# x rows staged in U's memory, W kept split in scratch, and loads placed steps ahead of their splits in a two-layer FNet and H3 kernel

## The chip, the cores and the metric

The kernel runs on one core of one Trainium2 chip. The metric is the device time of one execution in microseconds. The kernel before took 1289.1 us (median of 3 runs, 1285.89 to 1290.16).

## The reference

Two kinds of sublayer alternate, each with a residual and a layer norm in front: an FNet mixing layer (a) and a gated long convolution (b). S = 2048, D = 576, all float32.

```
x = x + A(layernorm(x));  x = x + B(layernorm(x), k, v, ...)     # twice

def A(x):                                   # Real(DFT_seq(DFT_hidden(x)))
    a = x @ dft_hid_re.T;  b = x @ dft_hid_im.T
    return dft_seq_re @ a - dft_seq_im @ b

def B(q):
    k_shift = causal 4-tap depthwise convolution of k with shift_k
    kv = k_shift * v
    y = long causal convolution of kv with ssm_k over S (by FFT of length 2S)
    return q * (y + kv * ssm_D)
```

B's convolution depends on k, v and weights alone, so it is the same in both rounds and is computed once.

## The kernel before, in words

Rows are laid out as 16 tiles j of 128 partitions x 576. Matrix products must be nearly float32 exact: every operand is split into a high part h (ScalarE, an ACTIVATE that rounds to float32r) and a low part l (VectorE, a subtraction: `split`, lines 76 to 78), and a product is three matmuls, hh, hl and lh. All matmuls are recorded under line 63, all such splits under lines 77 and 78; other lines name themselves. TensorE (PE) runs 6320 matmuls, of 512 or 288 columns.

The order is made by a list scheduler that places instructions on the five in-order engine queues from the program's order and its own estimates. SyncE (SP) issues nearly all loads and stores, in order: a load that must wait for a free buffer holds back everything behind it on that queue. `load_after` (line 128) only keeps a load behind an earlier one.

**First A layer** (`layer`, lines 265 to 301, called at 555): 128 steps n = (tb, g, k), 4 blocks tb of 512 output columns, g the real or imaginary sequence matrix C, k the 16 row tiles. A step is 14 matmuls: 12 into four accumulators s and 2 into rm for the last 64 columns of D. C tiles (256 KB) are loaded and split two steps ahead (`load_c`). In the first 16 steps the row tiles X[k] are made as they are needed: `load_x` (509) loads x into the ring "res", which has two slots of 576 words in `flts`; `get_x0` (514) asks for row j+1, takes the layer norm of row j (statistics on VectorE for the first eight rows, lines 141 to 155; on ScalarE for the others, 495 to 505; the power -0.5 on POOL) and splits it into X[j] (`to_x`, 157: rounding at line 159, low part at 161 and 162). After steps 15 and 31 and so on the accumulators are split into U, nine tiles of the transformed block in their own part `UT` of the tile `mats` (`evac_u`, `evac_r`). `hidden` (241) then multiplies U with the nine chunks of the hidden matrix W: 27 matmuls of 288 columns per half row tile, 216 for a block's four row tiles. Its pieces are spread over the steps after W_END, one a step (`finish`).

**Beside it** runs `branch` (310), the convolution of B, paced by `want` (556 to 561) in pieces per step: F1 (32 items, ssm_k and kv for 16 j, 12 matmuls each, steps 0 to 42; the kv items are eight VectorE operations, 363 to 366), with results stored to DRAM (`t_d`); then the middle stage (64 groups, lines 404 to 452, 9 matmuls each), which reads `t_d` and writes `v_d`; then I2 (16 items, to step 112). F1 takes the memory regions A and B; W lives in region A afterwards, so `load_w` (197) fills it between F1's end and the hidden products, in steps 41 to 46, from two "res" slots. `copy_w` (188) copies W to DRAM scratch in steps 47 to 55, unsplit.

**Second A layer**: rows of the second layer are made in steps 113 to 127 (`get_x1`, 525). Its first block of 512 columns is again 32 steps (counted 128 to 159 below). In steps 144 to 159 `build` (602) makes sums of rows for the other three blocks, from y reloaded from DRAM (`build_load`, 593): four kp, each in four pieces (tiles T5, T6, T7, T4 and R), one piece a step, its loads one step ahead. The other three blocks use Strassen's scheme (`strassen`, 706): seven products m in the order 5, 1, 6, 2, 7, 3, 4, four steps kp each, C combinations loaded four steps ahead. All four blocks' U goes to DRAM (`u_d`). In the last Strassen block, at the end of a product, W is reloaded and split into freed rows of X, and U of blocks 0 and 1 is loaded and split into freed places (`load_u`, 687; loops at 792 to 798). Then the tail (802 to 807): four blocks of hidden products with the final gate and output (`gated`, 487), U of block tb + 2 loaded and split behind block tb.

Of the kernel before, what the change touches and what calls it, by code (L numbers as in the profile page):

```python
# [10 lines left out]
F32 = mybir.dt.float32  # L11
FR = mybir.dt.float32r
AF = mybir.ActivationFunctionType
OP = mybir.AluOpType
# [16 lines left out]
F1_END = 40  # L31
W_END = 46
MID_END = 96
# [5 lines left out]
WIDE = 2 * NT  # L39
KR = 4  # L40
STAT = 20
STATIC = 14
B_LOAD = 15
B_FROM = 16
CSB = 5
U_AT = J * 2 * D
C_AT = U_AT + 9 * WIDE
RT_AT = 8 + 4 * STAT
# [5 lines left out]
def fnet_h3_kernel(ctx: ExitStack, tc: tile.TileContext, x, c_mat, w_re, w_im, k_pad, v, shift_k,  # L54
# [29 lines left out]
    def flat(words, dt, name):  # L84
        return sb.tile([P, words], dt, tag=name, name=name)
# [31 lines left out]

    mats = flat(C_AT + 3 * WIDE, FR, "mats")
    xs = mats[:, :U_AT].rearrange("p (j n) -> p j n", j=J)
    UT = mats[:, U_AT:C_AT].rearrange("p (k a n) -> p k a n", k=9, a=2)  # L120
    flts = flat(FLT, F32, "flts")
    mhalf = flts[:, :1]
    lay(flts, 8, ("stat", STAT, 4), ("rt", NT, 1))
    lay(mats, C_AT, ("cs", WIDE, 3))
# [62 lines left out]

    def copy_w():
        for ch in range(9):
            if ch < 8:  # L190
                load_after(w_d[ch], (w_re if ch < 4 else w_im)[(ch % 4) * P:(ch % 4 + 1) * P, :])
            else:
                load_after(w_d[ch][:REM], w_re[NC * P:, :])
                load_after(w_d[ch][REM:], w_im[NC * P:, :])
            yield

    def load_w(im_sign, late=False):
        W.clear()
        for ch in range(9):
            if not late and ch == 0:  # L200
                wg = region_a(FR, "w").rearrange("p (k n) -> p k n", k=9)
            w = two(xs[:, ch] if late else wg[:, ch])
            if late:
                load_after(w[:, 1].bitcast(F32), w_d[ch])
                split_in(w[:, 0], w[:, 1])
            else:
                raw = ring["res"]()
                if ch < 8:
                    nc.sync.dma_start(raw, (w_re if ch < 4 else w_im)[(ch % 4) * P:(ch % 4 + 1) * P, :])
                else:  # L210
                    nc.sync.dma_start(raw[:REM], w_re[NC * P:, :])
                    nc.sync.dma_start(raw[REM:], w_im[NC * P:, :])
                for lo, hi, sg in ((0, P, 1 if ch < 4 else im_sign),) if ch < 8 else ((0, REM, 1), (REM, P, im_sign)):
                    if sg > 0:
                        split(w[lo:hi, 0, :], w[lo:hi, 1, :], raw[lo:hi])
                    else:
                        nc.scalar.activation(w[lo:hi, 0, :], raw[lo:hi], AF.Copy, scale=-1.0)
                        nc.vector.scalar_tensor_tensor(w[lo:hi, 1, :], raw[lo:hi], -1.0,
                                                       w[lo:hi, 0, :].bitcast(F32), op0=OP.mult,
                                                       op1=OP.subtract)  # L220
            W.append(w)
            yield

    U = {}

    def evac_u(g, ps, dc):
        u = UT[:, g * NC + dc]
        split(u[:, 0, :], u[:, 1, :], ps[dc])
        U[g * NC + dc] = u

    def evac_r(g, ps):
        if g == 0:
            U[8] = UT[:, 8]
# [76 lines left out]
    def branch():  # L310
        wt = []
        f1r = region_b(FR, "f1r")
        lay(f1r, 0, ("xf", 2 * D, 3), ("fc", 4 * P, 3))
        lay(flts, SC_AT + 3 * NT + 3 * D, ("so", D, 3))
        f1f = region_a(F32, "f1f")
        lay(f1f, 0, ("k", 2 * D, KR), ("wt", 2 * D, 2), ("tmp", D, 1), ("v", D, 2), ("land", D, 3))

# [68 lines left out]
        for j, src in todo:  # L386
# [5 lines left out]
            yield  # L392
        f1_products(*xf)
        m1 = region_b(FR, "mid")
        lay(m1, 0, ("df", 2 * D, 3), ("yf", D, 3), ("mc", 4 * P, 1))
        fresh("res")
        lay(flts, SC_AT + 3 * NT, ("res", D, 2), ("kk", D, 2), ("pp", D, 1), ("vo", HD, 3))
# [111 lines left out]
    def load_x(j):  # L509
        if j < J:  # L510
            XL[j] = ring["res"]()
            nc.sync.dma_start(XL[j], x[:, j, :])
# [27 lines left out]
    pending = []  # L540
    lay(flts, SC_AT, ("craw", NT, 3), ("res", D, 2), ("junk", D, 1))
    br = branch()
    wl, wc = load_w(-1), copy_w()
    load_x(0)
    if PRE == 1:
        get_x0(0)
    for used in range(1, K_FIRST + 1):
# [7 lines left out]
    for n in layer(get_x0, lambda j: x[:, j, :], done0, pending):  # L555
        if n <= F1_END:
            want = K_FIRST + (F1_16 * n // 16 if n <= 16 else F1_16 + (32 - K_FIRST - F1_16) * (n - 16) // (F1_END - 16))
        elif n <= MID_END:
            want = 32 + 64 * (n - F1_END) // (MID_END - F1_END)
        else:  # L560
            want = min(113, 96 + 17 * (n - MID_END) // (I2_END - MID_END))
# [8 lines left out]
        if W_END < n <= W_END + 9:  # L570
            next(wc, None)
        m = n - PREP
        if m == 0:
            lay(flts, SC_AT + 3 * NT + 2 * D, ("xa", D, 2), ("yb", D, 2))
            lay(region_b(F32, "gate"), 0, ("xa", D, 3), ("yb", D, 3))
        if 0 <= m < TB * (TB - 1):
            get_x1(m)
    T, R, t7 = {}, {}, []

    def t_slot(m, kp):  # L580
        n = 4 * (m - 4) + kp
        return mats[:, U_AT + n * WIDE:U_AT + (n + 1) * WIDE] if n < 9 else t7[0][:, (n - 9) * WIDE:(n - 8) * WIDE]

# [17 lines left out]

    def build(kp, halves, rems):
        (b11, b12), (b21, b22) = ((t[:, :, :H], t[:, :, H:]) for t in halves)
        nc.vector.tensor_tensor(b22, b22, b12, OP.subtract)
# [6 lines left out]
        keep(7, kp, b22)  # L611
        nc.vector.tensor_tensor(rems[1], rems[1], rems[0], OP.subtract)
        t = two(t7[0][:, 7 * WIDE + kp * 4 * REM:7 * WIDE + (kp + 1) * 4 * REM])
        split(t[:, :, :REM], t[:, :, REM:], rems[1])
        R[kp] = t
        yield
# [69 lines left out]

    def load_u(tb, chs):
        for ch in chs:
            at = hu_slots[tb % 2][ch]
            t = two(t_slot(*at) if ch < 3 or tb % 2 == 0 else xs[:, at, :2 * NT])  # L690
            load_after(t[:, 1, :].bitcast(F32), u_d[tb][ch])
            split_in(t[:, 0, :], t[:, 1, :])
            HU[tb, ch] = t

# [73 lines left out]
    for n in layer(get_x1, lambda j: xb_d[j], done1, pending, 1):  # L768
        finish(pending, 1)
        if n == STATIC:  # L770
# [12 lines left out]
            ring["cs"].tiles.extend([free, *held])  # L783
        if n >= B_LOAD and (n - B_LOAD) % 4 == 0 and len(loaded) < KP:
            loaded.append(build_load(len(loaded)))
# [6 lines left out]
    wl = load_w(1, True)  # L792
    for tb, m, kp in strassen():
        if tb == TB - 1 and kp == KP - 1:
            for _ in range({1: 4, 6: 4, 3: 1}.get(m, 0)):
                next(wl)
            load_u(0, {6: range(4), 2: range(4, 8), 7: (8,)}.get(m, ()))
            load_u(1, {7: range(3), 3: range(3, 9)}.get(m, ()))
# [82 lines left out]
```

## Time and profile before

| What | Value |
|---|---|
| Median of 3 runs | 1289.1 us (1285.89 to 1290.16) |
| Profiled execution, its own time | 1285.66 us |
| Its span, first to last instruction | 1283.8 us |
| Mean granted TensorE clock | 0.983 |
| PE busy | 1210.0 us (94%), 6320 matmuls |
| DVE / ACT busy | 866.5 us (67%) / 634.4 us (49%) |
| DMA moved | 252.97 MB, mean 197 GB/s |
| W loads (9 + 1 transfers), each | 288 KB, 3.7 to 4.2 us to landing |
| U reloads | 256 KB, 5.2 to 5.4 us to landing |
| Reload of W from scratch | 9 of 288 KB, 4.9 us to landing |

A row of the profile's groups or waits names engine and line: "PE s L63 <- ACT mats L159" is PE, about to write s, released by ScalarE's instruction of line 159 that wrote mats; then the total, the number of times and the longest, in us. A timeline row has start, length, engine, line, operation, out<-in, shapes, count, and in brackets the idle time of the engine before it with what ended it. "q" behind an engine is its sequencer, where DMAs are issued. Matmul ends are modelled, and a busy PE may be a slow one.

### The profile page before, as it was taken

The page shows a single profiled execution, that of the slowest core. Times are in us where ns is not written, and L with a number is a line of the kernel's source. Part 1 is how long each engine was busy: PE and PEld are TensorE (multiplying, and loading weights), DVE is VectorE, ACT ScalarE, POOL GpSimd, SP SyncE. Part 2 cuts the span into 40 slices and gives each one's busy share as a digit, 9 for nine tenths or more (in the row PEclk, how much of TensorE's full clock was granted, in tenths as well). Part 3 has the DMA queues.
Part 4 walks back from the last instruction along what each step waited for, and adds up shares of the span by engine and source line. Part 5 has one row for each costly group of instructions (what it writes and reads, how often), then busy time and mean ns, then how long its engine had stood idle before and what let it go on. Part 6 is the DMA issues. An engine that isn't in the chain of part 4 may idle for free.

```text
span 1283.8 us, 18285 instructions
## 1 busy us (share of the span) xinstructions
PE 1210.0 (94%) x6320; PEld 1038.0 (81%) x6320; DVE 866.5 (67%) x1596; ACT 634.4 (49%) x1255; POOL 73.8 (6%) x102
## 2 busy tenths in 40 slices
PE   6689999999999999999998899999999999989997
PEld 5468888798789987788887788788877777779997
DVE  6867888547885588783257865665667667774664
ACT  4475565727884588874364332434443444560110
POOL 1110000000000000000012311000000000000111
PEclk9789999999999999999999999999999999999999
DMA  9557988736544455536798853675375476496631
GB/s 317 181 163 233 310 261 260 252 130 201 153 138 134 143 161 151 159 117 219 235 296 283 265 192 131 211 240 166 105 253 181 118 254 209 158 306 208 207 136 46
DMA packets 140670, 252.97 MB, mean 197 GB/s; under 512 B 15361, under 2 KB 39937, under 8 KB 140418
## 3 DMA queue, kind: packets, MB, share of 16 engines
q1 hardware_dynamic: 101698, 200.42, 49.3%
q10 hardware_dynamic: 33984, 42.48, 9.4%
q0 software_dynamic: 4896, 8.92, 2.6%
q8 instruction: 49, 0.80, 0.3%
q14 instruction: 43, 0.35, 0.1%
HBM read 190.42 MB, written 64.00 MB: 198 GB/s over the span
## 4 chain that ended last, share of the span: by engine, by line
PE 65%; DMA 11%; DVE 9%; ACT 8%; issue 3%; POOL 2%; SPq 0%; ACTq 0%; POOLq 0%; DVEq 0%
PE s L63 33%; PE bk L63 26%; PE rm L63 5%; DMA ph<-in_c_mat 3%; DMA t<-flts 2%; ACT mats L77 2%; DVE mats L78 1%; POOL flts L148 1%; ACT mid L77 1%; DVE flts L145 1%; DMA flts<-in_c_mat 1%; DMA mid<-t 1%; DMA flts<-in_x 1%; ACT flts L438 1%; ACT flts L419 1%
## 5 line engine op out<-in xcount | busy, mean ns | idle before, releaser
L63 PE MATMUL s<-mats 128*128 128x512 f32 x2292 | 589.3, 400 | 31.9 <-ACT mats L159 19.4
L63 PEld LDWEIGHTS s<-mats 128*128 128x128 f32 x2292 | 430.9, 192 | 123.5 <-ACT mats L159 22.5
L77 ACT ACTIVATE mats<-flts 128x512 fp32r<-128x512 f32 (+1 forms) x225 | 140.2, 626 | 163.8 <-PE rm L63 105.4
L78 DVE TENSOR_TENSOR mats<-flts,mats 128x512 fp32r<-128x512 f32 (+1 forms) x225 | 153.6, 685 | 58.7 <-ACT mats L77 57.2
L63 PEld LDWEIGHTS bk<-mid 128*128 128x128 f32 x768 | 111.4, 189 | 34.6 <-ACT flts L438 10.4
L63 PE MATMUL bk<-mid 128*128 128x288 f32 x768 | 126.2, 302 | 13.1 <-ACT flts L438 4.4
L63 PE MATMUL bk<-w,mats 128*128 128x288 f32 x864 | 121.6, 295 | 1.1 <-ACT flts L438 0.9
L63 PEld LDWEIGHTS bk<-w,mats 128*128 128x128 f32 x864 | 117.9, 188 | 3.6 <-ACT flts L438 1.4
L78 DVE TENSOR_TENSOR mid<-mid 128x576 fp32r<-128x576 f32 x96 | 72.4, 756 | 57.5 <-ACT mid L77 56.7
L63 PE MATMUL rm<-mats 128*128 128x512 f32 x338 | 106.6, 392 | 0.0
L77 ACT ACTIVATE mid<-mid 128x576 fp32r<-128x576 f32 x96 | 65.4, 684 | 73.9 <-DMA mid<-vd 41.7
L63 PE MATMUL s<-t,mats 128*128 128x512 f32 x384 | 96.9, 390 | 0.7 <-DVE ph L762 0.7
L63 PE MATMUL bk<-mats 128*128 128x288 f32 (+1 forms) x580 | 92.4, 305 | 0.0
L63 PEld LDWEIGHTS s<-t,mats 128*128 128x128 f32 x384 | 71.8, 188 | 16.3 <-ACT t L77 1.1
L63 PEld LDWEIGHTS bk<-mats 128*128 128x128 f32 x580 | 82.6, 189 | 2.5
L148 POOL TENSOR_TENSOR flts<-flts 128x1 f32<-128x1 f32 x56 | 49.1, 879 | 605.7 <-DVE flts L147 603.3
L63 PEld LDWEIGHTS rm<-mats 128*128 128x128 f32 x338 | 64.0, 190 | 13.5
L63 PE MATMUL bk<-f1r 128*128 128x288 f32 x384 | 62.1, 306 | 12.1 <-ACT f1r L77 7.5
L63 PEld LDWEIGHTS bk<-f1r 128*128 128x128 f32 x384 | 57.2, 195 | 18.2 <-ACT f1r L77 7.9
L380 ACT ACTIVATE flts<-bk 128x288 f32<-128x288 f32 x128 | 48.5, 409 | 24.1 <-DMA t<-flts 14.3
L77 ACT ACTIVATE mats<-ph 128x512 fp32r<-128x512 f32 x45 | 27.9, 628 | 44.5 <-DVE ph L672 19.3
L63 PE MATMUL bk<-mats,t 128*128 128x288 f32 x336 | 49.4, 295 | 0.0
(118 smaller groups left out, 1327.9 us busy)
## 6 DMA issues: line engine op xcount, KB each, us to landing
flts<-in_c_mat SPq DMA_DIRECT2D x150, 256.0 KB, 3.4
ph<-in_c_mat SPq DMA_DIRECT2D x48, 512.0 KB, 4.1
t<-flts ACTq DMA_DIRECT2D x64, 288.0 KB, 4.3
mid<-t SPq DMA_DIRECT2D x64, 288.0 KB, 2.8
flts<-in_c_mat SPq DMA_DIRECT2D x36, 512.0 KB, 4.4
flts<-in_x SPq DMA_DIRECT2D x32, 288.0 KB, 3.3
vd<-flts ACTq DMA_DIRECT2D x64, 144.0 KB, 2.9
mid<-vd SPq DMA_DIRECT2D x32, 288.0 KB, 4.1
```

Of the source, the lines that this page charges most:

```text
L63: nc.tensor.matmul(ps, lhsT, rhs, start=first, stop=last, skip_group_check=more)
L77: nc.scalar.activation(h, src, AF.Copy)
L78: nc.vector.tensor_tensor(l, src, h.bitcast(F32), OP.subtract)
L145: nc.vector.bn_stats(st[:, i, :], src[:, i * HD:(i + 1) * HD])
L148: pows.append(nc.gpsimd.tensor_tensor(rs, ve, mhalf, OP.pow).ins)
L380: nc.scalar.activation(so[:, c, :], ps[:, :HD], AF.Copy)
L419: nc.scalar.activation(kk[hi, 0, :], pk[lo, :HD], AF.Copy)
L438: nc.scalar.activation(vo, pv[:, :HD], AF.Copy)
```

## The change

- U's nine tiles move out of `mats` into a tile of their own, region "ru". In the first pass, before U exists, the same memory is an "x" ring of eight row slots and two "junk" slots; `get_x0` asks for row j+2, and two rows are loaded at the start.
- The room that x had in `flts` goes to F1: its outputs `so`, two `v` buffers and `tmp`; F1 gets one more split buffer (4), one more k buffer (KR = 5).
- W is loaded in steps 41 to 43, three chunks a step, through five slots "wl" (the memory of `so` and `v`); W_END is 43 and the hidden products may begin one step after. From step 60 on, every second step stores one split chunk, 576 KB, to scratch. In the last Strassen block W comes back already split (`reload_w`), with the sign of its imaginary half, so `split_u` negates the matching chunks of U.
- The middle stage begins at step 44, with the same end: 64 groups over 53 steps. `branch` has one more stop between F1 and the middle stage.
- `build` runs two pieces a step from step 146 on, each kp in two steps, loads two steps ahead, the remainder (R) first.
- Loads of U and their splits are separate: in the last Strassen block U of block 0 is loaded piece by piece from its step 2 on and split two steps later; W chunks follow from step 6 on. In the tail U of block tb + 1 is loaded before block tb's products and split in three groups behind its row tiles.

```diff
-W_END = 46
+W_END = 43
+W_SAVE = 60
-KR = 4
+KR = 5
-B_FROM = 16
+B_FROM = 18
+X_RING = 8
...
-    mats = flat(C_AT + 3 * WIDE, FR, "mats")
+    mats = flat(X_END + 3 * WIDE, FR, "mats")
...
+    def region_u(dt, name):
+        return sb.tile([P, 9 * WIDE], dt, tag="ru", name=name)
+    early = region_u(F32, "early")
+    lay(early, 0, ("x", D, X_RING), ("junk", D, 2))
...
-    w_d = [dr.tile([P, D], F32, name=f"wd{ch}") for ch in range(9)]
+    w_d = [dr.tile([P, 2 * D], F32, name=f"wd{ch}") for ch in range(9)]
...
+    def load_w():
+        lay(flts, SC_AT + 3 * NT, ("wl", D, 5))
+        wg = region_a(FR, "w").rearrange("p (k n) -> p k n", k=9)
         for ch in range(9):
+            w = two(wg[:, ch])
+            raw = ring["wl"]()
...
             W.append(w)
             yield
+        for ch in range(9):
+            load_after(w_d[ch], wg[:, ch].bitcast(F32))
+            yield
+
+    def reload_w(ch):
+        load_after(xs[:, ch].bitcast(F32), w_d[ch])
+        W[ch] = two(xs[:, ch])
...
-        lay(f1r, 0, ("xf", 2 * D, 3), ("fc", 4 * P, 3))
-        lay(flts, SC_AT + 3 * NT + 3 * D, ("so", D, 3))
+        lay(f1r, 0, ("xf", 2 * D, 4), ("fc", 4 * P, 3))
+        lay(flts, SC_AT + 3 * NT, ("so", D, 3), ("v", D, 2), ("tmp", D, 1))
...
     def load_x(j):
         if j < J:
-            XL[j] = ring["res"]()
+            XL[j] = ring["x"]()
             nc.sync.dma_start(XL[j], x[:, j, :])
     def get_x0(j):
         if X[j] is None:
-            load_x(j + 1)
+            load_x(j + 2)
...
-            want = 32 + 64 * (n - F1_END) // (MID_END - F1_END)
+            want = 33 + 64 * max(0, n - W_END) // (MID_END - W_END)
...
         if F1_END < n <= W_END:
-            for _ in range(-(-9 // (W_END - F1_END))):
+            for _ in range(3):
                 next(wl, 0)
+        if n >= W_SAVE and n % 2 == 0:
+            next(wl, 0)
...
-    def load_u(tb, chs):
+    def load_u(tb, ch):
...
+    def split_u(tb, ch):
+        t = HU[tb, ch]
+        for lo, hi, sg in ((0, P, 1 if ch < 4 else -1),) if ch < 8 else ((0, REM, 1), (REM, P, -1)):
...
         if n >= B_FROM:
-            if (n - B_FROM) % 4 == 0 and len(builds) < KP:
+            if (n - B_FROM) % 2 == 0 and len(builds) < KP:
                 builds.append(build(len(builds), *loaded[len(builds)]))
             next(builds[-1], None)
+            next(builds[-1], None)
+        if n == B_LOAD or n >= B_FROM and (n - B_FROM) % 2 == 0 and len(loaded) < KP:
+            loaded.append(build_load(len(loaded)))
...
+    for ch in range(9):
+        first = ch + 2 if ch < 4 else ch + 6 if ch < 8 else 18
+        at_step.setdefault(first, []).append((load_u, (0, ch)))
+        at_step.setdefault(first + 2, []).append((split_u, (0, ch)))
+        at_step.setdefault(6 + ch if ch < 8 else 22, []).append((reload_w, (ch,)))
...
     for tb in range(TB):
         us = [HU.pop((tb, ch)) for ch in range(9)]
-        pending.extend([us, tb, jj, lambda j: xb_d[j], done1, True] for jj in range(TB))
-        finish(pending, 99)
-        if tb + 2 < TB:
-            load_u(tb + 2, range(9))
+        for ch in range(9 if tb + 1 < TB else 0):
+            load_u(tb + 1, ch)
+        for jj in range(TB):
+            pending.append([us, tb, jj, lambda j: xb_d[j], done1, True])
+            finish(pending, 99)
+            for ch in range(3 * jj, min(9, 3 * jj + 3) if tb + 1 < TB else 0):
+                split_u(tb + 1, ch)
```

More of the change, by code (lines that the diff above doesn't have):

```diff
@@ L43 @@
 B_LOAD = 15
-B_FROM = 16
+B_FROM = 18
+X_RING = 8
 CSB = 5
-U_AT = J * 2 * D
-C_AT = U_AT + 9 * WIDE
+X_END = J * 2 * D
 RT_AT = 8 + 4 * STAT
@@ L116, in two @@
         return v.rearrange("p (a n) -> p a n", a=2)
-    mats = flat(C_AT + 3 * WIDE, FR, "mats")
-    xs = mats[:, :U_AT].rearrange("p (j n) -> p j n", j=J)
-    UT = mats[:, U_AT:C_AT].rearrange("p (k a n) -> p k a n", k=9, a=2)
+    mats = flat(X_END + 3 * WIDE, FR, "mats")
+    xs = mats[:, :X_END].rearrange("p (j n) -> p j n", j=J)
+    def region_u(dt, name):
+        return sb.tile([P, 9 * WIDE], dt, tag="ru", name=name)
+    early = region_u(F32, "early")
+    lay(early, 0, ("x", D, X_RING), ("junk", D, 2))
+    um = []
     flts = flat(FLT, F32, "flts")
@@ L123, in fnet_h3_kernel @@
     lay(flts, 8, ("stat", STAT, 4), ("rt", NT, 1))
-    lay(mats, C_AT, ("cs", WIDE, 3))
+    lay(mats, X_END, ("cs", WIDE, 3))
     anchor, stored, pows = [], [], []
@@ L197, in load_w @@
[L197 to L209, printed above, removed]
-                else:
[L211 to L220, printed above, removed]
@@ new lines, in load_w @@
+                nc.sync.dma_start(raw[:REM], w_re[NC * P:, :])
+                nc.sync.dma_start(raw[REM:], w_im[NC * P:, :])
+            for lo, hi, sg in ((0, P, 1 if ch < 4 else -1),) if ch < 8 else ((0, REM, 1), (REM, P, -1)):
+                if sg > 0:
+                    split(w[lo:hi, 0, :], w[lo:hi, 1, :], raw[lo:hi])
+                else:
+                    nc.scalar.activation(w[lo:hi, 0, :], raw[lo:hi], AF.Copy, scale=-1.0)
+                    nc.vector.scalar_tensor_tensor(w[lo:hi, 1, :], raw[lo:hi], -1.0,
+                                                   w[lo:hi, 0, :].bitcast(F32), op0=OP.mult,
+                                                   op1=OP.subtract)
@@ L221, in load_w, with ut @@
             W.append(w)
             yield
+        for ch in range(9):
[4 more added lines that the diff above has]
+        W[ch] = two(xs[:, ch])
     U = {}
+    def ut(ch):
+        return um[0][:, ch * WIDE:(ch + 1) * WIDE].rearrange("p (a n) -> p a n", a=2)
     def evac_u(g, ps, dc):
-        u = UT[:, g * NC + dc]
+        if not um:
+            um.append(region_u(FR, "u"))
+        u = ut(g * NC + dc)
@@ L232, in evac_r @@
         if g == 0:
-            U[8] = UT[:, 8]
+            U[8] = ut(8)
         lo, other = (0, REM) if g == 0 else (REM, 0)
@@ L312, in branch @@
         f1r = region_b(FR, "f1r")
[L313 to L314 removed]
+        lay(f1r, 0, ("xf", 2 * D, 4), ("fc", 4 * P, 3))
+        lay(flts, SC_AT + 3 * NT, ("so", D, 3), ("v", D, 2), ("tmp", D, 1))
         f1f = region_a(F32, "f1f")
[L316 removed]
+        lay(f1f, 0, ("k", 2 * D, KR), ("wt", 2 * D, 2), ("land", D, 3), ("v", D, 1))
         def load_w4():
@@ L393, in branch @@
         f1_products(*xf)
+        yield
         m1 = region_b(FR, "mid")
         lay(m1, 0, ("df", 2 * D, 3), ("yf", D, 3), ("mc", 4 * P, 1))
-        fresh("res")
         lay(flts, SC_AT + 3 * NT, ("res", D, 2), ("kk", D, 2), ("pp", D, 1), ("vo", HD, 3))
@@ L540, in fnet_h3_kernel @@
     pending = []
-    lay(flts, SC_AT, ("craw", NT, 3), ("res", D, 2), ("junk", D, 1))
+    lay(flts, SC_AT, ("craw", NT, 3))
     br = branch()
-    wl, wc = load_w(-1), copy_w()
+    wl = load_w()
     load_x(0)
-    if PRE == 1:
-        get_x0(0)
+    load_x(1)
     for used in range(1, K_FIRST + 1):
@@ L558, in fnet_h3_kernel @@
         elif n <= MID_END:
-            want = 32 + 64 * (n - F1_END) // (MID_END - F1_END)
+            want = 33 + 64 * max(0, n - W_END) // (MID_END - W_END)
         else:
-            want = min(113, 96 + 17 * (n - MID_END) // (I2_END - MID_END))
+            want = min(114, 97 + 17 * (n - MID_END) // (I2_END - MID_END))
         while used < want:
@@ L565, in fnet_h3_kernel @@
         if F1_END < n <= W_END:
-            for _ in range(-(-9 // (W_END - F1_END))):
+            for _ in range(3):
                 next(wl, 0)
+        if n >= W_SAVE and n % 2 == 0:
+            next(wl, 0)
         if n > W_END:
             finish(pending, 1)
-        if W_END < n <= W_END + 9:
-            next(wc, None)
         m = n - PREP
@@ L581, in t_slot @@
         n = 4 * (m - 4) + kp
-        return mats[:, U_AT + n * WIDE:U_AT + (n + 1) * WIDE] if n < 9 else t7[0][:, (n - 9) * WIDE:(n - 8) * WIDE]
+        return um[0][:, n * WIDE:(n + 1) * WIDE] if n < 9 else t7[0][:, (n - 9) * WIDE:(n - 8) * WIDE]
     def keep(m, kp, src, sign=1):
@@ L602, in build @@
     def build(kp, halves, rems):
+        nc.vector.tensor_tensor(rems[1], rems[1], rems[0], OP.subtract)
+        t = two(t7[0][:, 7 * WIDE + kp * 4 * REM:7 * WIDE + (kp + 1) * 4 * REM])
+        split(t[:, :, :REM], t[:, :, REM:], rems[1])
+        R[kp] = t
         (b11, b12), (b21, b22) = ((t[:, :, :H], t[:, :, H:]) for t in halves)
@@ L611, in build @@
         keep(7, kp, b22)
[L612 to L615, printed above, removed]
         yield
@@ L685, in fnet_h3_kernel @@
                 [(7, 1), (7, 2), (7, 3)] + list(range(9, 15)))
-    def load_u(tb, chs):
[L688 to L693, printed above, removed]
+    def load_u(tb, ch):
+        at = hu_slots[tb % 2][ch]
+        t = two(t_slot(*at) if ch < 3 or tb % 2 == 0 else xs[:, at, :2 * NT])
+        load_after(t[:, 1, :].bitcast(F32), u_d[tb][ch])
+        HU[tb, ch] = t
+    def split_u(tb, ch):
+        t = HU[tb, ch]
+        for lo, hi, sg in ((0, P, 1 if ch < 4 else -1),) if ch < 8 else ((0, REM, 1), (REM, P, -1)):
+            h, l = t[lo:hi, 0, :], t[lo:hi, 1, :]
+            if sg > 0:
+                split_in(h, l)
+            else:
+                raw = l.bitcast(F32)
+                nc.scalar.activation(h, raw, AF.Copy, scale=-1.0)
+                nc.vector.scalar_tensor_tensor(l, raw, -1.0, h.bitcast(F32), op0=OP.mult, op1=OP.subtract)
     steps = [(tb, m, kp) for tb in range(1, TB) for m in ORDER for kp in range(KP)]
@@ L783, in fnet_h3_kernel @@
             ring["cs"].tiles.extend([free, *held])
-        if n >= B_LOAD and (n - B_LOAD) % 4 == 0 and len(loaded) < KP:
-            loaded.append(build_load(len(loaded)))
         if n >= B_FROM:
-            if (n - B_FROM) % 4 == 0 and len(builds) < KP:
+            if (n - B_FROM) % 2 == 0 and len(builds) < KP:
                 builds.append(build(len(builds), *loaded[len(builds)]))
             next(builds[-1], None)
+            next(builds[-1], None)
+        if n == B_LOAD or n >= B_FROM and (n - B_FROM) % 2 == 0 and len(loaded) < KP:
+            loaded.append(build_load(len(loaded)))
         if n >= 30:
             ahead(n - 29, 0)
[L792 to L798, printed above, removed]
+    at_step = {}
+    for ch in range(9):
[3 more added lines that the diff above has]
+        at_step.setdefault(6 + ch if ch < 8 else 22, []).append((reload_w, (ch,)))
+    for n, (tb, m, kp) in enumerate(strassen()):
+        if tb == TB - 1:
+            for act, args in at_step.get(n - (TB - 2) * 28, ()):
+                act(*args)
     fresh("res", "yb")
```

6 lines of the change are left out of this document (1 added, 5 removed).

## The prediction

> **What bounds the kernel now.** I read the page first, then busy time in stretches of 25 us, then who waited for whom, then the timeline.
>
> ```profile
> span 1283.8 us, 18285 instructions
> PE 1210.0 (94%) x6320; PEld 1038.0 (81%) x6320; DVE 866.5 (67%) x1596; ACT 634.4 (49%) x1255; POOL 73.8 (6%) x102
> PEclk9789999999999999999999999999999999999999
> ```
>
> TensorE (PE) does the work, but its 94% hides slow matmuls. Where nothing disturbs it, the chain of waits has 12 matmuls of 512 columns in 2.72 us (0.2267 each) and 12 of 288 in 1.58 us (0.1317). The kernel has 3440 and 2880 of them: 780 + 379 = 1159 us. So 125 us of the span are not needed by the matmuls. I subtracted, step by step (a step ends with its two matmuls into rm), this price from the time passed. Lost: 12.8 us before the first step ends at 19.3; 34.5 in steps 1 to 15 (to 105.1); 3.0 in steps 16 to 40; 7.9 in 41 to 47; 16.3 in 48 to 63 and 72 to 95 together; 2.0 between them; 5.9 in 96 to 113; 13.5 in 114 to 127; 4.7 in step 144; by 25 us stretches some 3.3, 4.4 and 8.1 in the three Strassen blocks; the rest at the end.
>
> ```profile
> 0.00:25.00 25.00, 14.85 (x53) 12.03 (x54) 15.71 (x37) 12.40 (x22) 4.02 (x9) 1.00 0.91 314
> 25.00:50.00 25.00, 16.20 (x58) 11.73 (x59) 20.78 (x52) 10.08 (x15) 4.87 (x6) 0.83 0.64 212
> 50.00:75.00 25.00, 18.79 (x68) 14.59 (x66) 21.46 (x44) 16.01 (x34) 3.11 (x4) 0.83 0.62 187
> 75.00:100.00 25.00, 21.64 (x82) 16.57 (x82) 11.61 (x33) 17.83 (x36) 5.39 (x9) 0.86 0.60 177
> ...
> 175.00:200.00 25.00, 25.00 (x135) 21.73 (x134) 24.70 (x38) 17.06 (x38) 1.59 (x3) 1.00 0.85 265
> ```
>
> Columns: the stretch, then PE, weight loads, VectorE (DVE), ScalarE (ACT), POOL, the granted clock, DMA share, GB/s. In the first 100 us nothing is full for long: a chain of latencies.
>
> ```profile
> SPq L512 <- DVE mats L162: 27.1, 14, 3.9
> PE s L63 <- ACT mats L159: 19.4, 9, 5.5
> DVE flts L145 <- DMA flts<-in_x: 4.9, 3, 2.8
> ```
>
> That is the chain: PE waits for a row's rounding (L159); the row's load stands on SyncE's queue until the split of an older row (L162) frees one of two slots (14 times, 27.1 us). Rows therefore come in pairs: steps 4, 6, 8, 10 and 14 lose 7.3, 5.9, 5.2, 5.5 and 3.8 us, 27.7 of the 34.5.
>
> ```profile
> 38.16 4.54 PE L63 MATMUL s<-mats 128*128 128x512 f32 x12 [5.52 <-ACT mats L159]
> 42.99 2.88 PE L63 MATMUL s<-mats 128*128 128x512 f32 x12
> ...
> 818.87 0.69 DVE L604 TENSOR_TENSOR flts<-flts 128x512 f32<-128x512 f32 x1 [4.47 <-DMA flts<-y]
> ...
> 1128.69 0.63 ACT L77 ACTIVATE mats<-mats 128x512 fp32r<-128x512 f32 x1 [4.68 <-DMA mats<-ud]
> ```
>
> Each pair gap also halves the clock: the 12 matmuls behind it took 4.54 us, against 2.88 next. The two last lines are the other waits that the change aims at: an operand build and a U split, each queued directly behind a load that had not landed.
>
> **1. x rows in U's memory (first pass).** The two-slot wait goes. In the built order of the changed kernel SyncE issues x0, x1, then x2 to x6 together as its 9th to 13th transfers. What is left is work in order on VectorE. Its queue up to the last row's split holds 33 F1 products and sums x 0.75 = 24.8, five F1 splits x 0.75 = 3.7, 16 C splits x 0.685 = 11.0, 16 row splits x (0.685 + 0.22) = 14.5, 16 half statistics x 0.452 = 7.2, small ones 8.2, one more 0.7: 70.1 us. It can start at 3.7. Before the first row's split, which stands behind 12.6 us of it and more statistics than today (15.7 today), I walk the queue to 18.7: 6.1 idle. 70.1 + 6.1 + 2 us of matmuls behind the last split = 78: the near end. PE's own sum is lower: first step done at 19.6 by the same walk, then 15 x 3.17 + 27 x 0.1317: 70.7. So are the bytes: 23.4 MB moved by 105 us, at the 314 GB/s of the first stretch 74.5. The far end: VectorE's idle rows up to 105 us add to 33, 4.9 of them for x; the 28 others stay, 10 of them in the first 19 us already counted: 78 + 18 = 96. I take 85, nearer to 78, because most of those waits are for ScalarE, which itself waited for rows; ScalarE's own work from 28 us on is 46 us (eight rows at 3.36, 12 C roundings at 0.63, the rest F1), nearly as long as VectorE's, so some interlock remains. **-20** (-27 to -9).
>
> On the clock, the row first: at 95.25 us a gap of 1.95 us was followed by 12 matmuls in 4.61. The Trainium skill (TensorE: Matmul & The Clock Gate, What's actually happening) lets the clock halve after an idle window of about 3.4 us; the trace shows the half clock behind a shorter gap that followed others. By the rule alone, five gaps cut under 3.4 us would return 5 x 1.7 = 8 us even if they did not close; by the row they must close.
>
> **2. Steps 16 to 40.** PE's order is the same. VectorE has 8 F1 operations and 2 splits fewer done by then: 7.5 us deferred. From 100 to 225 it is busy 18.1 to 24.7 of each 25 us, 102.6 of 125, so that fits; **0** (to +7.5 without that cover).
>
> **3. W in one go.** Five landing slots (the F1 output and v buffers) take the place of two. Today the last W split ends at 260.5 and the hidden products start at 265.9. In the new order the last W loads stand on SyncE behind the first reads of F1's result, which wait for its last store (240.4 today); the last is issued by 243, lands in 4.2, is split in 0.7 + 0.8: 249. Steps 43 to 45 cover PE to 248.6. Of the 6.6 lost in steps 44 to 47 some 1.5 stay: **-5** (-6.6 to +2, if the ring's second round waits for the first's splits).
>
> **4. Middle stage.** Its 64 groups now lie in 53 steps, not 56. A step with two groups loses 1.0 us and the two after it 0.7 each, since ScalarE and VectorE are at 20 to 22 of 25 us there. Outside the hidden products there are five such steps now and eight in the new order: 3 x 2.4 = 7, less the 2.5 lost in steps 48 to 51, the ramp behind today's W stage: **+4** (0 to +9, if two more steps of each doubled one are slowed by 0.3). W's nine saves of 576 KB lie on SyncE between these reads, where the DMA share is 0.52; the DRAM copies (nine of 288 KB) go: 0.
>
> **5. Build.** The y loads stay at step 15's place, their use moves from step 144 to 146, 6.35 us later; the wait was 4.47 on VectorE and cost PE 4.7. Each build is packed into two steps: 4 x 0.69 + 4 x 0.68 + 0.5 = 6.0, with two C splits 7.4 of VectorE in 6.35, four times: 4.2 us late at the end, covered by five free steps before Strassen. **-4** (-4.7 to +4.2).
>
> **6. Last Strassen block and tail.** Out go nine W splits (9 x 0.68 ScalarE, 9 x 0.76 VectorE); U splits come two steps (5 to 7 us) behind loads that take 5.2 to 5.4. The loss of 8.1 falls towards the 4.4 of the block before; but W comes back as nine 576 KB loads (double), on the queue of the C loads that set those 4.4: two of them, 2 us each, fall among those. **-2** (-5 to +3). The tail gets nine more splits per block (9 x 0.69 in 28.4 us, VectorE now 14 to 17 of 25): 0; without cover +6.
>
> Sum: -20 - 5 + 4 - 4 - 2 = -27. From the profiled execution's 1285.7 us (span 1283.8 plus 1.9): 1258.7. The median shown, 1289.1, is 3.4 above it: **1262**.
>
> **Rivals.** *Given back in F1 (20%).* The deferred 7.5 us are not absorbed: for it speak VectorE at 24.70 of 25 in 175 to 200; against, the 18.1 to 21.7 of the other stretches. 1262 + 7.5, and 1.7 for one half-clock group: 1271.
>
> *Transfers crowd (with the former).* Five x rows (1.47 MB) stand ahead of C and k loads: at 314 GB/s 4.7 us late once: 1267. The Trainium skill (DMA: Bandwidth & Descriptors, Issuing engines are not separate DMA queues) says that all queues share 16 engines and interleave; the first stretch's share of 0.91 agrees.
>
> *The ring does not matter (5%).* Only 4.9 us of direct waits on x stand in the list; if VectorE and ScalarE, alternating, set the pace, step 15 stays at 105: 1262 + 20 = 1282.
>
> *Slower (7%): VectorE's queue packed too early.* One mechanism: work not yet due (eight rows' statistics, two builds' steps) stands in order ahead of work that is. First row 3.0 late, 7.5 of F1 owed, row pace as now: +10.5; the build's cover used up, its 4 lost: 1289.1 + 10.5 - 5 + 4 + 0 - 2 = 1297. It decides once the gain of the first pass is under 3 us. Against it: the walk finds rows 2 to 7 ready ahead of PE.
>
> **How the numbers follow.** 68% for the forecast (own range 1250 to 1268). The near ends together give -43 (1246), not all at once; the range 1248 to 1277 takes in nearly all of that and the first two rivals. The last two rivals (12%) are left out, and some 6% at its edges. A measurement tells 0.3% (3.9 us) from no change: faster 0.90, same 0.03 (between the last two), slower 0.07.
>
> **What will show it.** Right: step 15 ends near 85, clock near 1.0 from 25 to 100 us, no SyncE wait for L162; hidden products start near 250; no gap at step 144; eight doubled middle steps at 2.4. Wrong: step 15 over 96, losses in steps 17 to 40, PE waiting for C loads more than 5 us in the last Strassen block.

## The result, and the profile after

The changed kernel takes 1258.0 us (median of 4 runs, 1256.74 to 1259.47), the kernel before 1288.8 (median of 4, 1285.89 to 1290.16): a ratio of 0.9764, 95% interval 0.9743 to 0.9786. The forecast was 1262 in a range of 1248 to 1277. Its profiled execution took 1256.88 us. A profile shows one execution, which can lie some us off its kernel's median; where that matters below, its own time is given.

The head of its page: span, TensorE's busy time, and the granted clock over 40 slices.

```profile
span 1254.0 us, 18238 instructions
PE 1193.0 (95%) x6320; PEld 1027.0 (82%) x6320; DVE 860.0 (69%) x1591; ACT 631.9 (50%) x1250; POOL 73.8 (6%) x102
PEclk9999999999999999999999999999999999999999
```

The "7" and "8" at the start of the clock's row are gone, and PE is busy 17 us less for the same 6320 matmuls. Next the changed kernel's first 100 us by stretches; the columns are as before (stretch, PE, weight loads, VectorE, ScalarE, POOL, clock, DMA share, GB/s).

```profile
0.00:25.00 25.00, 14.80 (x60) 12.24 (x61) 16.81 (x57) 15.56 (x25) 5.69 (x14) 1.00 0.92 313
25.00:50.00 25.00, 23.43 (x110) 19.45 (x109) 23.71 (x57) 21.39 (x48) 5.56 (x7) 1.00 0.96 325
50.00:75.00 25.00, 23.76 (x109) 19.29 (x108) 23.66 (x49) 20.86 (x42) 6.23 (x7) 1.00 0.80 269
75.00:100.00 25.00, 24.93 (x133) 21.26 (x132) 24.64 (x37) 13.54 (x31) 1.06 (x2) 1.00 0.89 269
```

From 25 us on PE and VectorE are both nearly full. PE handles 109 or 110 records in a stretch where it had 58 and 68. The chain of latencies has become two nearly full engines. In the changed kernel's list of waits up to 80 us, SyncE's long wait of before (14 times, 27.1 us) is down to one, and PE hardly waits for rows (total, times, longest):

```profile
PE bk L64 <- ACT f1r L78: 9.8, 1, 9.8
...
PE s L64 <- DVE mats L170: 1.2, 1, 1.2
...
SPq L518 <- DVE mats L170: 3.5, 1, 3.5
```

The 9.8 us are the start of the program: the first load of ssm_k and its split (ScalarE waits 7.8 us for that load).

Where the time went, from step end to step end in the profiled executions. "Ring alone" and "best" are e1 and e8 below; the time of a stretch includes matmuls that were moved into it. Behind step 159 the count goes on by pairs of matmuls into rm: steps 160 to 168 are the first Strassen block up to its last product. What a step "loses" is, as in the prediction, its time less 0.2267 us for each matmul of 512 columns and 0.1317 for each of 288.

| Stretch | before | after | ring alone (e1) | best (e8) |
|---|---|---|---|---|
| to the end of step 15 | 105.1 | 74.1 | 73.6 | 74.1 |
| steps 16 to 40 (F1) | 121.7 | 123.7 | 122.5 | 123.3 |
| steps 41 to 95 (W, middle) | 332.7 | 336.1 | 330.8 | 327.5 |
| steps 96 to 143 | 260.1 | 258.6 | 261.6 | 257.7 |
| steps 144 to 159 (build) | 55.4 | 55.7 | 55.2 | 50.7 |
| steps 160 to 168 | 80.3 | 80.7 | 80.5 | 80.4 |
| from there to PE's end | 322.0 | 318.5 | 321.3 | 317.3 |

The stretch to step 15 gives 31.0 us, as much as the whole change (29.8 in the spans). The rest of the table nearly cancels, though the forecast had put 7 us of gain there.

### The profile page after: what moved, and what is told of

Its sections match the earlier page's. It is cut to its first block, busy times and chain, and to the rows that moved or that the text cites. A ratio compares the mean times of both kernels' runs of the same rounds, so it can differ in the third digit from the quotient of the medians.

```text
span 1254.0 us, 18238 instructions
## 1 busy us (share of the span) xinstructions
PE 1193.0 (95%) x6320; PEld 1027.0 (82%) x6320; DVE 860.0 (69%) x1591; ACT 631.9 (50%) x1250; POOL 73.8 (6%) x102
## 4 chain that ended last, share of the span: by engine, by line
PE 68%; DMA 10%; DVE 9%; ACT 8%; issue 3%; POOL 1%; ACTq 0%; SPq 0%; POOLq 0%; DVEq 0%
PE s L64 35%; PE bk L64 27%; PE rm L64 6%; DMA ph<-in_c_mat 3%; DMA flts<-in_c_mat 2%; DVE mats L79 2%; DMA t<-flts 1%; DVE flts L153 1%; POOL flts L156 1%; ACT mats L78 1%; ACT mid L78 1%; DMA mid<-t 1%; ACT flts L444 1%; DVE ph L677 1%; ACT flts L425 1%
## 5 line engine op out<-in xcount | busy, mean ns | idle before, releaser
L64 PE MATMUL s<-mats 128*128 128x512 f32 x2094 | 525.8, 392 | 14.3 <-DVE mats L79 7.9
L64 PEld LDWEIGHTS s<-mats 128*128 128x128 f32 x2094 | 384.6, 188 | 91.6 <-DVE mats L79 10.8
L78 ACT ACTIVATE mats<-flts 128x512 fp32r<-128x512 f32 x209 | 130.8, 626 | 148.2 <-PE rm L64 100.0
L79 DVE TENSOR_TENSOR mats<-flts,mats 128x512 fp32r<-128x512 f32 x209 | 142.6, 684 | 58.6 <-ACT mats L78 58.1
L64 PE MATMUL bk<-w,u 128*128 128x288 f32 x864 | 123.0, 296 | 3.2 <-ACT w L78 1.2
L64 PEld LDWEIGHTS bk<-w,u 128*128 128x128 f32 x864 | 118.0, 188 | 7.1 <-ACT w L78 1.6
L64 PE MATMUL s<-t,mats 128*128 128x512 f32 x258 | 64.4, 389 | 0.0
L64 PE MATMUL bk<-mats 128*128 128x288 f32 (+1 forms) x340 | 56.7, 309 | 0.0
L64 PE MATMUL s<-mats,u 128*128 128x512 f32 x198 | 50.3, 389 | 1.9 <-DVE ph L776 1.9
L64 PEld LDWEIGHTS bk<-mats 128*128 128x128 f32 x340 | 48.8, 188 | 2.0
```

What stands on the lines that cost most here:

```text
L64: nc.tensor.matmul(ps, lhsT, rhs, start=first, stop=last, skip_group_check=more)
L78: nc.scalar.activation(h, src, AF.Copy)
L79: nc.vector.tensor_tensor(l, src, h.bitcast(F32), OP.subtract)
```

## The experiments

Ratios are to the kernel before, on the same chip.

**Is it the ring, and the ring alone?** e1 is the kernel before with part 1 only; e2 and e3 are the changed kernel with a shallower ring.

```diff
 # e1: the kernel before, with
+    early = region_u(F32, "early")
+    lay(early, 0, ("x", D, X_RING), ("junk", D, 2))
...
-            XL[j] = ring["res"]()
+            XL[j] = ring["x"]()
...
-            load_x(j + 1)
+            load_x(j + 2)
 # e2: the changed kernel, with
-X_RING = 8
+X_RING = 2
...
-            load_x(j + 2)
+            load_x(j + 1)
 # e3: the changed kernel, with
-X_RING = 8
+X_RING = 3
```

> The kernel before with the x ring alone (eight row slots in U's memory, row j+2 asked for). Theory: the ring alone brings the whole gain of the first pass, so step 15 ends near 75 instead of 105.1 and the time is 1288.8 - 30 = 1259 (F1's rings are the old ones, so up to 3 us less). Rival: the ring needs F1's new buffers (xf 4, k 5, outputs out of the way) to bring it; then step 15 ends between 85 and 100 and the time is 1270 to 1284. If the rest of the change is worth the -3 that the step ends of the two profiles leave over (F1 +2, W -3.5, middle +3, build 0, last block -3), the changed kernel is 0 to 3 us faster than this one.

> The changed kernel with the ring cut to two slots and row j+1 asked for, as before; all other parts stay. Theory: the gain of the first pass goes, step 15 ends at 100 to 106 and the time is 1258 + 27 to 31, 1285 to 1289. Rival: F1's new buffers brought part of it; then step 15 ends at 85 to 95 and the time is 1268 to 1278.

> The changed kernel with three row slots and row j+2 asked for. Theory (a load stood on SyncE's queue until the split of the row that freed its slot; one more slot lets it leave a whole row earlier): most of the gain stays, step 15 ends at 76 to 82, time 1260 to 1266. Rival: only a deep ring takes the latencies out; three slots end step 15 at 88 to 98, time 1272 to 1282.

| | time, us | ratio (95%) | step 15 ends at |
|---|---|---|---|
| e1, before + ring of 8 | 1254.6 | 0.9734 (0.9701 to 0.9766) | 73.6 |
| e2, after, 2 slots | 1290.3 | 1.0014 (0.9991 to 1.0037) | 107.5 |
| e3, after, 3 slots | 1267.6 | 0.9843 (0.9810 to 0.9875) | 85.3 |
| after, 8 slots | 1258.0 | 0.9764 (0.9743 to 0.9786) | 74.1 |

Both directions agree. The ring without the rest has the whole gain, and the rest without the ring has none. F1's new buffers are not needed for it. The profiled execution of e2 took 1297.9 us, 7.6 above its median, so its 107.5 may be high by some of that.

e3 fell between its two theories. It has one slot more than e2 and also asks for a row one step earlier (row j+2), so the two come together. SyncE's wait for slots is the same in both shallow rings, 21.4 and 21.5 us. First e3's, then e2's list of SyncE's waits:

```profile
SPq L518 <- DVE mats L170: 21.4, 13, 3.7
```

```profile
SPq L518 <- DVE mats L170: 21.5, 13, 4.0
```

What differs is what PE pays for it. PE's waits for a row in e3, then in e2:

```profile
PE s L64 <- ACT mats L167: 7.2, 6, 3.9
```

```profile
PE s L64 <- ACT mats L167: 20.7, 7, 6.0
```

My reading is that the third slot lets a row wait ready ahead of PE, so that the same late load no longer reaches PE. The queue's own wait total is no price; PE's wait behind it is. e2's steps 2, 4, 6, 10 and 14 lose 3.9, 6.2, 6.9, 6.8 and 8.3 us, the pairs of before; e3's lose 5.9 and 3.8 in steps 3 and 7 and at most 1.6 in any other.

**Does VectorE's queue set the first pass?** The forecast's near end, 78, summed VectorE's work. e4 adds to it.

```diff
...
+            h = X[j].bitcast(F32)
+            nc.vector.tensor_tensor(X[j][:, D + REM:], src[:, :NC * P], h[:, :NC * P], OP.subtract)
```

> The changed kernel with the low part of each first-layer row computed twice (16 more VectorE subtractions of 128x512, 0.68 us each, 10.9 in all; the result is the same). If VectorE's queue sets the pace of the first pass, as the prediction's floor of 78 had it (70.1 us of its work in order), step 15 ends 9 to 11 us later, at 83 to 85, time 1267 to 1269. Rival, which the early end at 74.1 speaks for: PE's own matmuls set it (70.2 us with 3.9 lost in steps 1 to 15) and VectorE's sum was counted too high; then step 15 ends 0 to 4 later and the time is 1258 to 1262.

Measured: 1264.0 us (1261.25 to 1273.6), ratio 0.9824 (0.9775 to 0.9873). In the profiled execution, which took 1273.6 us, step 15 ends at 78.1, 4.0 later. Step 40 ends at 209.1, 11.3 later: steps 16 to 40 lose 13.0 us against 4.9. So the pace up to step 15 is mostly not VectorE's, as the rival had it; but what VectorE does not finish there it owes to F1. By step 40 the added 10.9 us had come back whole in that execution; the medians differ by 6. The prediction's "7.5 us deferred, so that fits" leaves little room to spare.

Why the sum of 70.1 was too high is seen in VectorE's timeline in the changed kernel (start, length, engine, line, operation):

```profile
48.42 0.75 DVE L369 TENSOR_TENSOR flts<-f1f 128x576 f32<-128x576 f32 x1
49.09 0.75 DVE L79 TENSOR_TENSOR f1r<-f1f,f1r 128x576 fp32r<-128x576 f32 x1
49.76 0.22 DVE L169 TENSOR_TENSOR mats<-early,mats 128x64 fp32r<-128x64 f32 x1
49.90 0.68 DVE L170 TENSOR_TENSOR mats<-early,mats 128x512 fp32r<-128x512 f32 x1
50.50 0.75 DVE L371 TENSOR_TENSOR f1f<-f1f,flts 128x576 f32<-128x576 f32 x1
```

Each instruction starts 0.08 us before the one ahead has ended: 0.67 for a listed 0.75, 0.60 for 0.68, 0.14 for 0.22. Up to the end of the last row's split, at 69.5 us, the trace of the changed kernel lists about 69.5 us of VectorE instructions, near the forecast's 70.1, but VectorE is busy for only 58.7 us of that time: nearly every instruction overlaps the one ahead. Some 11 us of the 70.1 do not exist. The Trainium skill (VectorE: DVE Perf Modes, Two Vector instructions with no wait between them) says that only some instructions, by where their operands start, are held until all earlier ones have finished; by that rule the instructions above were not held.

**Do the middle's doubled steps cost what was said?** e5 keeps all 64 groups in the same 53 steps, and moves the doubling to steps that have hidden products.

```diff
-            want = 33 + 64 * max(0, n - W_END) // (MID_END - W_END)
+            want = 33 + max(0, n - W_END) + sum(i <= n for i in (45, 46, 47, *range(64, 72)))
```

> The changed kernel with the same 64 middle groups over the same 53 steps, but the eleven steps that take two groups put into 45 to 47 and 64 to 71, where PE also has hidden products to do (9.1 us a step and more), none among the steps of 4.4 us. Theory (a doubled step costs about 2.4 us because ScalarE and VectorE have no room in a 4.4 us step): the losses of steps 48 to 63 and 72 to 95 fall from 20.4 to 7 to 12, those of 64 to 71 stay at 4 to 6, and the time is 1258 - 8 to -12, 1246 to 1250. Rival (the losses there are ScalarE's and VectorE's total, or the DMA's, and follow the groups wherever they lie): steps 64 to 71 take up what the others give; time 1255 to 1259.

Measured: 1242.2 us (1241.47 to 1249.43), ratio 0.9656 (0.9617 to 0.9694). That is 15.7 less than the changed kernel, more than expected. Steps 48 to 63 and 72 to 95 lost 7.0 + 13.3 = 20.4 us in the changed kernel; in e5 1.9 + 4.3 = 6.2. Steps 64 to 71 went from 4.7 to 6.5. Another 2.9 came from steps 144 to 159, which this edit does not touch. A doubled step thus cost (20.4 - 6.2) / 8 = 1.8 us among steps of 4.4 us. Beside hidden products it cost about 0.6: steps 65 to 71, all doubled in e5, lose 0.6 to 0.8 each, where the changed kernel's single steps among them lose 0.1 to 0.4 and its doubled one, step 69, 0.7. Step 64 loses 1.8 in e5 and 3.3 in the changed kernel. In the timeline of the changed kernel one of them (step 73) looks so:

```profile
414.22 1.35 PE L64 MATMUL bk<-mid 128*128 128x288 f32 x9
417.02 0.66 PE L64 MATMUL bk<-mid 128*128 128x288 f32 x3 [1.45 <-ACT flts L444]
417.52 1.33 PE L64 MATMUL s<-mats 128*128 128x512 f32 x5
```

PE wants a bank for the second group while ScalarE is still emptying one for the first (L444). That wait is the largest in the list, and a good third of what is lost there. PE's waits for that line from step 72 to 95, in the changed kernel and then in e5:

```profile
PE bk L64 <- ACT flts L444: 4.8, 9, 1.4
```

```profile
PE bk L64 <- ACT flts L444: 0.3, 1, 0.3
```

**Why did the build's move bring nothing?** Steps 144 to 159 lose 4.9 us in the changed kernel, 4.7 before, all of it in step 144. The timeline of the changed kernel there, VectorE's lines, then ScalarE's and PE's:

```profile
785.11 0.69 DVE L79 TENSOR_TENSOR mats<-flts,mats 128x512 fp32r<-128x512 f32 x1
791.16 0.69 DVE L613 TENSOR_TENSOR flts<-flts 128x512 f32<-128x512 f32 x1 [5.37 <-DMA flts<-y]
791.77 0.68 DVE L79 TENSOR_TENSOR mats<-flts,mats 128x512 fp32r<-128x512 f32 x1
```

```profile
791.89 0.63 ACT L78 ACTIVATE t<-flts 128x512 fp32r<-128x512 f32 x1 [5.28 <-DVE flts L613]
...
794.83 1.07 ACT L646 ACTIVATE ph<-s 128x512 f32<-128x512 f32 x2
```

```profile
791.90 0.61 PE L64 MATMUL rm<-mats 128*128 128x512 f32 x2
795.46 4.58 PE L64 MATMUL s<-mats 128*128 128x512 f32 x12 [2.95 <-ACT ph L646]
```

The y loads are issued from 784.11 on and take 2.1 to 6.6 us to landing; the first subtraction can start at 791.16. The program's order puts the build's first subtraction (L613) two steps after its load, but the scheduler placed it on VectorE right behind the C split of 785.11, where it stood for 5.37 us with C splits queued behind it. ScalarE stood behind it in turn, and the eviction of s (L646) behind ScalarE, for which PE waited 2.95 us. The next 12 matmuls took 4.58 us; the granted clock was 0.53 from 798.0 to 800.1 us. e6 forbids that place and moves no load: `csplit[-1]` is VectorE's instruction of the newest C split in program order, and VectorE's instructions of the block stay behind it on the queue.

```diff
+            with tc.issue_after(csplit[-1]):
-            next(builds[-1], None)
-            next(builds[-1], None)
+                next(builds[-1], None)
+                next(builds[-1], None)
```

> The changed kernel with each build step's VectorE instructions held in queue behind the newest C split of program order, so that the first of them cannot stand directly behind the y load on VectorE's queue. Theory (steps 143 to 159 lose 4.9 because the scheduler put the build's first subtraction ahead of the C splits, where it waited 5.4 us for its load): the loss falls to 0.5 to 2 and the time to 1253.5 to 1255.5. Rival (the load is late for whatever comes first, or the packed build then comes late for Strassen): the loss moves on to steps 148 to 162, time 1257 to 1260.

Measured: 1252.0 us (1250.84 to 1257.27), ratio 0.9721 (0.9689 to 0.9754). In e6's timeline step 143 ends at 794.6 and the subtraction starts 2.4 us behind that, where the changed kernel had it 1.3 ahead of it; it stands behind the splits that PE needs, and nothing waits:

```profile
794.48 2.20 PE L64 MATMUL s<-mats 128*128 128x512 f32 x9
...
797.00 0.68 DVE L613 TENSOR_TENSOR flts<-flts 128x512 f32<-128x512 f32 x1
```

Steps 144 to 159 lose 0.0 us, and nothing moved on to the steps behind (160 to 168: 2.2, against 2.8). In e8, e9 and e10, which have the tie too, they lose 0.0 as well; the eight kernels without it lose 2.0 to 4.9 there. So the place is settled by the traces. The gain in the whole time is less certain. The median's 6.0 is larger than the 4.9 that were lost there, within the two intervals, but e6's profiled execution took 1257.27 us, no less than the changed kernel's: it takes 322.7 us from step 168 to PE's end, against 318.5. The tie is not what slows that part, since e8, with the same instructions in the same order there on every engine, takes 317.3.

**Was it the lead of the U splits in the last Strassen block?** e7 puts U's splits of block 0 directly behind their loads; e10, on top of e8, puts loads and splits back to the ends of products.

```diff
 # e7
-        at_step.setdefault(first + 2, []).append((split_u, (0, ch)))
+        at_step.setdefault(first, []).append((split_u, (0, ch)))
 # e10, on top of e8, with the line of e7 too
-        first = ch + 2 if ch < 4 else ch + 6 if ch < 8 else 18
+        first = 11 if ch < 4 else 15 if ch < 8 else 19
```

> The changed kernel with block 0's U splits put directly behind their loads in the last Strassen block instead of two steps later. Theory (the two steps are what takes the waits away): 2 to 5 us come back in that block, time 1260 to 1263. Rival (the scheduler places the splits where it thinks the loads have landed, whatever the program's order, or the waits are hidden by C splits already done ahead): no difference, 1257 to 1259.

> e8 with U of block 0 loaded and split at the ends of products 6, 2 and 7 of the last Strassen block, in lumps of four, four and one, as before; W still comes back split and U of block 1 still in the tail. If the lead of U's loads is what took the 3.5 us wait out of the last block (PE behind ScalarE behind a U load), 3 to 5 us come back there: 1245 to 1247. Rival (W kept split and block 1's U moved to the tail did it, 18 of 27 splits gone from this block): 0 to 1 us, 1242 to 1243.

e7: 1257.1 us (1256.87 to 1263.51), ratio 0.9757 (0.9725 to 0.9789): no difference, the rival. The two steps between load and split in the program's text do nothing by themselves. e10: 1244.8 us (1238.89 to 1248.1), ratio 0.9653 (0.9623 to 0.9683), where e8 has 0.9635 (0.9605 to 0.9665). The intervals overlap and the median lies between the two theories, so the times leave it open. From step 168 to PE's end e10 takes 319.9, e8 317.3, but e6, with e8's instructions there in the same order, takes 322.7, so that difference shows nothing. The lists of waits give the place. e10's has a new line near the end of the block, 1075 to 1110 us:

```profile
PE s L64 <- DMA t<-ud: 3.1, 1, 3.1
```

In the changed kernel PE's wait in the same place was 1.54 us, where it had been 3.48. First the changed kernel, then the kernel before:

```profile
1101.67 0.73 PE L64 MATMUL s<-mats,t 128*128 128x512 f32 x2 [1.54 <-ACT mats L78]
```

```profile
1129.89 0.88 PE L63 MATMUL s<-mats,t 128*128 128x512 f32 x2 [3.48 <-ACT mats L77]
```

The four kernels that load U at the ends of products (the kernel before, e1, e9, e10) wait 2.9 to 3.5 us there, the eight with the early loads 1.4 to 2.1. So it is where the U loads stand that counts for this wait, by 1 to 2 us; a gain in the whole time is not shown.

**The two edits together (e8), and without W's and the last block's part (e9).** e9 is e1 with the eight doubled middle steps in 64 to 71 and the build tied, its pace of one piece a step kept.

> The edits of e5 and e6 together. If both theories hold their gains add: 1258 - 10 - 4 = 1244 (1241 to 1247), below the x ring alone (1254.6). If neither does, 1256 to 1259.

> The kernel before with the x ring (as in e1), the middle's eight double steps put into 64 to 71 and the build held behind the newest C split; W in six steps, copied unsplit and split again in the last Strassen block, U as before. It tells what W's part and the last block's part of the change are worth beside e8 (1242.0). By the step ends and the end part of the two profiles: W's part 1.7 to 3.5 (steps 41 to 47 lost 6.1 in e1, 4.4 in the changed kernel), the last block 3 (321.7 against 318.9 behind step 168): 1245 to 1249. Rival (W's early start only moves hidden products within the same work, and the last block's gain is used up elsewhere): 1240 to 1243.

e8: 1242.0 us (1239.99 to 1245.89), ratio 0.9635 (0.9605 to 0.9665), 16 us below the changed kernel and 12.5 below the ring alone. Its median is the lowest, but not to be told from e5's 1242.2: the tie adds nothing there that can be measured, since e5 lost only 2.0 in steps 144 to 159. The two gains do not add. Its page:

```profile
span 1237.9 us, 18249 instructions
...
PE 1187.9 (96%) x6320; PEld 1029.2 (83%) x6320; DVE 859.8 (69%) x1591; ACT 633.8 (51%) x1250; POOL 73.8 (6%) x102
```

e9: 1244.3 us (1239.18 to 1245.27), ratio 0.9642 (0.9615 to 0.9669). It can't be told from e8 by the times. What the last block's part is worth stays open: from step 168 on e9 takes 320.6 and e8 317.3, less far apart than e6 and e8 are there with the same instructions. W's early load shows no gain: steps 41 to 95 take 326.8 in e9, and 327.5, 326.1 and 326.4 in e8, e5 and e10, which load W early. Up to step 47 e8 loses 2.3 us less than e9 (5.4 against 7.7), in steps 48 to 71 2.4 more. e8's groups sit closer there; that this takes the gain back is a reading.

## Why the prediction was right, and where its steps were not

The time, the sign and the main term were right: the ring is the change. That the sum came within 4 us is partly chance, since its steps erred in both directions: the first pass gave 11 us more than said, and the rest cost 1 where 7 of gain were said.

- **x ring, -20 said, -31.0 in the profile.** The mechanism was right: no SyncE wait of note, no pairs, clock 1.00. The size was not: even the near end of 78 was passed. Two terms failed. VectorE's 70.1 us was a sum of listed lengths that overlap; the work took 58.7 us, and the forecast's idle time of 6.1 us beside it was 10.8. The step from 78 to 85, "some interlock remains", did not show: up to 74.1 us VectorE waits 1.3 us for ScalarE and 3.9 for POOL, and ScalarE 7.0 for VectorE. What was taken for the lower of two bounds, PE's own 70.7, was the nearer one: steps 1 to 15 lose 3.9 us.
- **Steps 16 to 40, 0 said, +2.0.** Whether deferred VectorE work caused it is not shown. At the end of step 15 the changed kernel has 43 of F1's 161 VectorE instructions done, the kernel before 49; but e1, with 43 too, loses 3.7 in these steps, and e2, with 58, loses 5.2, against 4.9 here and 3.0 before. Six kernels with this F1 and the ring of eight lose 4.0 to 6.4. The rival "given back in F1" did not come at its price; e4 shows that it can.
- **W, -5 said.** To step 47 the profile gives 3.5 of loss less, of 7.9. The hidden products start at 217.0, which with the 29 us gained earlier is 246 on the clock of before, so the walk to 249 was good. But e9, without it, loses as much in steps 41 to 95 as e8, so nothing of the 3.5 is left there; the middle's loss in the three steps given up for it is the likely reason, not a shown one.
- **Middle, +4 said, +6.8 of loss.** Outside the hidden products it came as said, +4.1: steps 48 to 63 lost 7.3 before and 7.0 after, though by the forecast's count one more doubled step stands there, so the credit for the ramp came; steps 72 to 95, with two more, lost 9.0 and 13.3. The price of 2.4 a doubled step stands against 1.8 by e5. What the forecast left out is steps 64 to 71, which lost 2.7 more, 2.3 of it in step 64 (1.0 before, 3.3 after).
- **Build, -4 said, +0.3.** The step that failed is "their use moves from step 144 to 146". It was taken from the program's text. The scheduler put the instruction behind its load as before, and the load was slow, 7 us from issue to the first use; e6 puts it where the text had it, and there the gain is.
- **Last block and tail, -2 said, -3.5.** The wait that it aimed at shrank from 3.48 to 1.54, as said. The stretch's 3.5 is of the size by which two executions of the same instructions differ there (318.5 in the changed kernel, 321.7 in e4), so the -2 is neither shown nor refuted. The tail's extra splits cost nothing: behind the last Strassen block PE loses 1.0 us in both kernels.

On the clock, the row and the rule: behind a wait of 2.95 us at 795.46, 12 matmuls took 4.58 us, where the undisturbed group takes 2.72. The Trainium skill (TensorE: Matmul & The Clock Gate, What's actually happening) asks for an idle window of about 3.4 us. Here, as before the change, a shorter gap was enough. The forecast's 1.7 us a group held in size (4.58 against 2.72 here), and in the first 100 us, where the gaps closed, the granted clock is 1.00 throughout.

The other rivals did not come: transfers did not crowd (325 GB/s from 25 to 50 us, and PE waits for no row's load there), the ring does matter, and VectorE's early work did not delay the first row (step 0 ends at 18.1, before at 19.3).

What stays open: why e6's median gained a little more than its step lost; what W's part and the last block's part are worth in the whole time; the 2.0 in steps 16 to 40; and steps 114 to 127, which lose about 12 to 14 us in every version (the second layer's first rows) and which this change does not touch.

## What to carry to other kernels

A load that waits for a slot on an in-order queue costs what the consumer runs out of, not what the queue waits: here one more slot, with rows asked for one step earlier, took away two thirds of it (step 15 ended at 107.5, then at 85.3 us), and the rest needed more depth. Sum an engine's queue by starts, not by lengths, before calling it the floor. And put the extra work of an uneven stage into the steps where the bound engine has the most of its own, and look in the built queue, not in the program's text, for where an instruction behind a load really stands.

## What was not expected of the hardware

VectorE's records overlap by about 0.08 us each where no wait stands between them: a listed 0.75 us starts its successor after 0.67. ScalarE's do the same, 0.63 us listed and 0.54 from start to start (1089.00 to 1089.54 in the changed kernel).
